# Three products of the first attention blocks moved one step in a hand-paced schedule

## The chip, the cores and the metric

One Trainium2 chip, one core of it. The metric is the device time of one execution in microseconds (us).

## The reference

An attention block feeds two feed-forward blocks. Only the first part touches the change:

```python
scores = scale * np.matmul(q, k.transpose(0, 1, 3, 2))       # B, H, S, D = 4, 8, 576, 64
bias = -(cum[:, :, :, None] - cum[:, :, None, :])            # cum: running sum of max(s, 0)
scores = np.where(causal, -1000000000.0, scores + np.minimum(bias, 0.0))
scores = scores - np.max(scores, axis=-1, keepdims=True)
attn = np.exp(scores)
attn = attn / (np.sum(attn, axis=-1, keepdims=True) + 1e-09)
out = np.matmul(attn, v)
```

The rows of `out`, 2304 tokens by 512, go through `x @ w_in`, `h - tanh(h)`, `@ w_out`, and then through `((x @ w1) * (x @ w2)) @ w3 @ w_out`.

## The kernel before, in words

Attention runs over 32 *pairs*: two heads of one batch entry, and either its first 256 query rows (kind A, one unit of work) or the other 320 (kind B, three units B1, B2, B3). The first eight pairs are batch entry 0: pairs 0 to 3 are its four A pairs, pairs 4 to 7 its B pairs. For every unit the kernel computes scores on TensorE (PE) into two PSUM banks, takes row maxima on VectorE (DVE), exponentials with row sums on ScalarE (ACT), transposes the result on PE, copies it out on ACT, and multiplies it with the values on PE (`products`, L313). The product with the values is not yet divided by the row sums. Those take their own way: `invert` (L330) makes reciprocals on DVE, `turn` (L336) transposes them on PE, `store` (L340) copies them out of PSUM on ACT (L343) and writes them to DRAM, `spread` (L347) reads them back with a DMA that repeats them over 64 partitions, into the tile `rb` (three buffers), and `finish` (L370) multiplies the two on DVE (L374), from PSUM into the tile `xy`, which the feed-forward blocks read.

The order of the work is written by hand, in steps. `at(step, order, fn, ...)` (L495) puts a piece of work into a step; pieces of a step go by their order number. A unit's scores stand in step k (order 4), its maxima in step k + 1 (order 1), its exponentials there too (2.5). Pairs 0 to 3 begin at steps 0, 2, 4, 6; pair 4 has its units at steps 8, 10, 12, pair 5 at 14, 16, 18. The products with the values of pairs 0 to 3 stand in steps 7, 9, 11, 13 at order 8, so at the end of the step. `finish` stands at order 2.6 in the step that L529 gives. Filling matmuls that compute nothing (`warm`, L213) stand in steps 1 to 12, the last nine of them in step 12 just ahead of the scores.

What this order binds differs by engine. PE runs its instructions exactly in it. ACT, DVE, GpSimd and SyncE's queue (SP) are ordered by a scheduler when the kernel is built: it plays the program through with its own estimates and lets an instruction go ahead of earlier ones if it finds it ready first. Two things hold it: data dependencies, and edges that are added by hand. `in_turn(i, other)` is such an edge: it says that i comes after `other` on its engine. `finish` puts one on its product, to `least[0]`, the last scale operation of the maxima (L261) that has been written so far. For pairs of batch entry 0, a unit's maxima end with such an operation, except B2, which takes a partial maximum that B3's step completes.

Two buffers tie `finish` to PE. For pairs 0 to 3 the products with the values go to one of two PSUM banks in turn, so pair 2's products (step 11) write the bank that pair 0's `finish` reads, and pair 3's (step 13) the bank of pair 1's:

```python
if p.first and p.early:
    p.pv = ps_y.tile([P, 512], F32, tag=f"y{p.n % 2}", name=f"pv{p.n}")
```

All other PSUM tiles of this stage (scores, transposes, reciprocals) share five banks. Pair 3's `finish` also cuts the first 256 columns of `xy` into high parts (ACT, L366) and low parts (DVE, L368), one set for each of the four pairs, which the first feed-forward block multiplies; the scheduler may run each as soon as its pair's product is there. The step of this `finish` is also what the planner takes as the begin of the first feed-forward block. Beside all this DVE and ACT convert weights, which arrive as raw 64-bit words by DMA (`raw_win`, `raw_wout`): three bit operations (L88, L91, L93), then a split into high (ACT, L64) and low part (DVE, L65).

Of the kernel before, what the change touches and what calls it, by code (L numbers as in the profile page):

```python
# [16 lines left out]
B, H, S, D = 4, 8, 576, 64  # L17
# [20 lines left out]
def tile_kernel(ctx: ExitStack, tc: tile.TileContext, qk, v, s, w_in, w_out, w1, w2, w3t, w_o2, outT):  # L38
# [84 lines left out]
    with ExitStack() as actx:  # L123
# [371 lines left out]
        def at(step, order, fn, *args):  # L495
            when.setdefault(step, []).append((order, len(when.get(step, ())), fn, args))
# [10 lines left out]
        for p in pairs:  # L507
            n, k0 = p.n, k
            lag = 5 if p.first and p.early else 7
            for m, j in enumerate(p.units):  # L510
                k = k0 + 2 * m
                for i in NEED[j]:
                    at(max(k - 2, start), 5, bias, p, i)
                    if not p.first:
                        at(max(k - 1, start + 1), 0.2, causal, p, i)
                at(k, 4, scores, p, j)
                at(k + 1, 1, minimum, p, j)
                at(k + 1, 2.5, exps, p, j)
                for e in range(2):
                    at(k + e + lag, 2, transposes, p, j, e)  # L520
                    at(k + e + lag + 1, 1.5, evacuate, p, j, e)
                at(k + lag + 2 + (not p.first), 8 if p.first else 3.9, products, p, j)
            ke = k0 + 2 * len(p.units) - 2
            k = ke + 2
            at(ke + 2, 5.5, invert, p)
            at(ke + 5, 2.4, turn, p)
            at(ke + 6, 1.2, store, p)
            at(ke + 6, 3.9, spread, p)
            fin = ke + lag + (5 if p.first and p.early else 3)  # L529
            at(fin, 2.6 if p.first else 4.05, finish, p)  # L530
            if p.hp == H // 2 - 1:
                avail.append((S * p.b + (BLK if p.early else S), fin))

            if n > 1 and (p.early or p.first):
                q = p if p.first else pairs[n + 1]
                at(max(k0 - 6, start + 1), 4.2, load, p, q, "load")
                at(max(k0 - 2, start + 1), 4.3, load, p, q, "load_v")
                if not p.first:
                    at(k0 - 5, 4.4, load, p, pairs[n + 1], "load_cum")
                    at(k0 - 3, 5.7, p.cut, pairs[n + 1])  # L540
# [529 lines left out]
```

## Time and profile before

| | |
|---|---|
| median of 3 runs | 920.8 us (920.65, 920.8, 923.38) |
| the profiled execution | 925.05 us |
| its span, first to last instruction | 923.3 us |
| mean granted TensorE clock | 0.996 |
| PE, DVE, ACT, POOL busy | 98%, 71%, 49%, 18% |
| chain that ended last, by engine | PE 80%, DVE 9%, DMA 6%, ACT 3% |

The span is one execution, followed by the hardware profiler. The chain is followed back from the last instruction: at each step to what released it, or to the instruction ahead of it on its engine. In the rows below L374 is the product in `finish`, L257 and L261 are the maxima and their scale operation, `s_B` are scores of a B pair, `pv` the products with the values, `spare` the filling matmuls. A bracket tells how long the engine had been idle before the row and what released it. PEclk 1.00 is 2.4 GHz, 0.50 is 1.2 GHz.

### The profile page before, as it was taken

The page shows a single profiled execution, that of the slowest core. Times are in us where ns is not written, and L with a number is a line of the kernel's source. Part 1 is how long each engine was busy: PE and PEld are TensorE (multiplying, and loading weights), DVE is VectorE, ACT ScalarE, POOL GpSimd, SP SyncE. Part 2 cuts the span into 40 slices and gives each one's busy share as a digit, 9 for nine tenths or more (in the row PEclk, how much of TensorE's full clock was granted, in tenths as well). Part 3 has the DMA queues.
Part 4 walks back from the last instruction along what each step waited for, and adds up shares of the span by engine and source line. Part 5 has one row for each costly group of instructions (what it writes and reads, how often), then busy time and mean ns, then how long its engine had stood idle before and what let it go on. Part 6 is the DMA issues. An engine that isn't in the chain of part 4 may idle for free.

```text
span 923.3 us, 16370 instructions
## 1 busy us (share of the span) xinstructions
PE 908.5 (98%) x6030; PEld 799.0 (87%) x6030; DVE 654.4 (71%) x1447; ACT 447.9 (49%) x1047; POOL 165.5 (18%) x170
## 2 busy tenths in 40 slices
PE   8999999999999999999999999999999999999998
PEld 5567788888888889998888888898999999999998
DVE  8787798877878766758987885867146647564555
ACT  4567888867776743334532341445224332523133
POOL 1004646554444400000000000000011111111100
PEclk9899999999999999999999999999999999999999
DMA  5655365454544523599787544346399877776874
GB/s 168 196 166 186 104 246 192 158 172 150 173 149 139 183 86 99 194 366 351 256 292 252 184 146 145 115 173 233 106 314 329 296 253 288 283 266 249 285 262 151
DMA packets 59936, 192.92 MB, mean 209 GB/s; under 512 B 6640, under 2 KB 21136, under 8 KB 55760
## 3 DMA queue, kind: packets, MB, share of 16 engines
q1 hardware_dynamic: 59856, 191.88, 60.0%
q8 instruction: 47, 0.77, 0.4%
q14 instruction: 33, 0.27, 0.1%
HBM read 148.71 MB, written 43.15 MB: 208 GB/s over the span
## 4 chain that ended last, share of the span: by engine, by line
PE 80%; DVE 9%; DMA 6%; ACT 3%; issue 1%; SPq 0%; DVEq 0%; ACTq 0%
PE h L117 10%; PE y L435 9%; PE W L875 9%; PE hb L117 9%; PE yb L117 9%; PE oW L938 5%; PE Y L875 5%; PE w3o L117 5%; PE pv L327 4%; PE oY L938 4%; PE s_B L229 4%; PE pt_B L301 3%; PE V L875 2%; DMA raw_w<-in_w3t 2%; DMA raw_wout<-in_w_out 1%
## 5 line engine op out<-in xcount | busy, mean ns | idle before, releaser
L117 PE MATMUL h<-xhl,win 128*128 128x256 f32 x864 | 120.6, 286 | 1.0 <-DVE xhl L368 0.7
L117 PEld LDWEIGHTS h<-xhl,win 128*128 128x128 f32 x864 | 105.8, 188 | 12.0 <-DVE pf_B L310 2.7
L117 PE MATMUL hb<-x,win 128*128 128x512 f32 (+1 forms) x480 | 104.5, 367 | 0.0
L117 PE MATMUL yb<-ghb,wout 128*128 128x512 f32 (+1 forms) x320 | 96.1, 368 | 1.0 <-ACT ghb L64 1.0
L117 PEld LDWEIGHTS hb<-x,win 128*128 128x128 f32 x480 | 83.9, 188 | 15.0
L206 POOL TENSOR_SCALAR pr<-cb,cq 128x384 f32<-128x384 f32 (+1 forms) x48 | 92.2, 1935 | 22.1 <-ACT pr L208 9.7
L1008 POOL TENSOR_TENSOR xy<-c,c 128x384 f32<-128x384 f32 x12 | 15.3, 1279 | 444.3 <-DVE c L997 444.3
L435 PE MATMUL y<-gh,wout 128*128 128x256 f32 x576 | 85.2, 287 | 0.9 <-DVE gh L64 0.9
L290 ACT ACTIVATE pr<-pr,nm 128x128 f32<-128x128 f32 (+2 forms) x120 | 71.5, 598 | 26.3 <-DVE nm L268 26.3
L435 PEld LDWEIGHTS y<-gh,wout 128*128 128x128 f32 x576 | 72.4, 188 | 4.2 <-issue 1.9
L117 PEld LDWEIGHTS yb<-ghb,wout 128*128 128x128 f32 x320 | 58.2, 188 | 11.5 <-ACT ghb L64 1.6
L117 PE MATMUL yb<-glb,wout 128*128 128x512 f32 (+1 forms) x160 | 58.5, 368 | 0.2 <-DVE glb L65 0.2
L301 PE MATMUL pt_B<-ident,pr 96*128 96x96 f32 (+1 forms) x384 | 50.8, 255 | 0.1
L268 DVE CUSTOM_DVE_ANT_0 pr<-s_B,pr 96x512 f32<-96x512 f32 (+1 forms) x72 | 44.3, 638 | 6.6 <-PE s_B L229 5.4
L64 ACT CAST ghb<-thb 128x512 fp32r<-128x512 f32 (+1 forms) x40 | 23.1, 578 | 50.4 <-DVE thb L737 49.7
L464 ACT ACTIVATE th<-h 128x256 f32<-128x256 f32 x72 | 26.9, 374 | 37.5 <-PE h L117 36.4
L435 PE MATMUL y<-gl,wout 128*128 128x256 f32 x288 | 45.0, 278 | 0.0
L218 POOL TENSOR_SCALAR_AFFINE_SELECT pr<-pr 128x256 f32<-128x256 f32 (+2 forms) x60 | 29.9, 521 | 82.9 <-issue 72.4
L301 PEld LDWEIGHTS pt_B<-ident,pr 96*128 96x128 f32 (+1 forms) x384 | 41.7, 143 | 2.2 <-issue 1.2
L886 ACT COPY s<-Y 128x384 f32<-128x384 f32 x24 | 11.6, 482 | 63.0 <-PE Y L875 60.6
L310 ACT COPY pf_B<-pt_B 128x512 f32<-128x512 f32 (+2 forms) x72 | 35.8, 499 | 10.0 <-PE pt_B L301 9.2
L990 DVE TENSOR_TENSOR c<-Y,u 128x384 f32<-128x384 f32 x24 | 13.3, 556 | 37.5 <-PE Y L875 37.4
(218 smaller groups left out, 2060.6 us busy)
## 6 DMA issues: line engine op xcount, KB each, us to landing
S<-wg_d SPq DMA_DIRECT2D x24, 1024.0 KB
wo<-wo_d SPq DMA_DIRECT2D x42, 512.0 KB
A<-wg_d SPq DMA_DIRECT2D x24, 768.0 KB
qk<-in_qk SPq DMA_DIRECT2D x16, 576.0 KB
raw_win<-in_w_in SPq DMA_DIRECT2D x16, 512.0 KB
raw_wout<-in_w_out SPq DMA_DIRECT2D x16, 512.0 KB
raw_w<-in_w SPq DMA_DIRECT2D x16, 512.0 KB
wg_d<-pks SPq DMA_DIRECT2D x8, 1024.0 KB
```

Source lines behind the costliest of these rows:

```text
L117: i = nc.tensor.matmul(ps, a, b, start=first and n == 0, stop=last and n == 2, skip_group_check=skip)
L206: nc.gpsimd.tensor_scalar(out=t[:pw, e, :w], in0=p.cb[:pw, e, :w], scalar1=c, scalar2=0.0, op0=ALU.add, op1=ALU.min)
L218: nc.gpsimd.affine_select(out=dg, in_=dg, pattern=[[0, 2], [-1, w - c]], compare_op=ALU.is_ge, fill=-8e9, base=0, channel_multiplier=1)
L229: latest[0] = nc.tensor.matmul(ps[e][:PW[i], o:o + k1 - k0], w[r, 0, CH0[i]:CH0[i] + PW[i]], x[r, 1, k0:k1], start=z == 0 and (not p.first ...
L268: least[0] = nc.vector.tensor_tensor_reduce(out=t[:pw, k0:k1], in0=ps[:pw, o:o + k1 - k0], in1=t[:pw, k0:k1], scale=-0.125, scalar=nm[:pw, ...
L290: last_exp[0] = nc.scalar.activation(t[:pw, :], t[:pw, :], AF.Exp, bias=m, scale=-1.0, accum_out=p.sums[:pw, e, c:c + 1])
L301: nc.tensor.transpose(pt[:, at:at + pw], p.pr[i][:pw, e, KC0[kj]:KC0[kj] + P], ident[:pw, :pw])
L310: (nc.vector.tensor_copy if j == "B2" and not p.first else nc.scalar.copy)(pf[:, :at], pt[:, :at])
L327: nc.tensor.matmul(p.pv[D * e:D * e + D, c:p.nq], p.vs[:, e, kj], pf[:, beg:end], start=z == 0, stop=z == len(todo) - 1, skip_group_check= ...
L435: nc.tensor.matmul(o, wout[f][:, z, P * c:P * c + P], x, start=f == 0 and n == 0 and c % 2 == 0, stop=f == F1 - 1 and n == 2, skip_group_c ...
L875: i = nc.tensor.matmul(ps[:, :T], w[:, x, P * j:P * j + P], b[:, y, j], start=first and j == n == 0, stop=stop and j == 1 and n == 2, skip ...
L938: nc.tensor.matmul(ps[:, :T], w[:, a, q % 2, P * j:P * j + P], x[:, b, q], start=o in ("B11", "B21", "T1") and q == z == 0, stop=o in ("T4 ...
```

## The change

The step of `finish` gets one added for the pairs whose `hp` (the pair's place in its batch entry) is below 3, if they are A pairs of batch entry 0. So pairs 0, 1 and 2 go from steps 10, 12 and 14 to 11, 13 and 15; pair 3 stays in step 16. Nothing else is edited.

```diff
-            fin = ke + lag + (5 if p.first and p.early else 3)
+            fin = ke + lag + (5 + (p.hp < H // 2 - 1) if p.first and p.early else 3)
             at(fin, 2.6 if p.first else 4.05, finish, p)
             if p.hp == H // 2 - 1:
                 avail.append((S * p.b + (BLK if p.early else S), fin))
```

Here `ke` is the step of the pair's last scores and `lag` is 5 for these pairs.

## Rows read from the trace of the kernel before

**Rows 1.** Page, part 1 (engine, busy us, share, instructions), whole span

```profile
PE 908.5 (98%) x6030; PEld 799.0 (87%) x6030; DVE 654.4 (71%) x1447; ACT 447.9 (49%) x1047; POOL 165.5 (18%) x170
```

**Rows 2.** Windows by stage, core 0 (PE, PEld, DVE, ACT, POOL busy, PEclk, DMA share, GB/s)

```profile
16.00:46.00 30.00, 27.85 (x155) 15.78 (x156) 22.54 (x58) 17.14 (x56) 0.00 (x0) 0.89 0.57 180
```

**Rows 3.** Windows of 1 us, same columns

```profile
36.00:37.00 1.00, 1.00 (x8) 0.75 (x9) 1.00 (x4) 0.00 (x0) 0.00 (x0) 0.50 0.40 158
...
42.00:43.00 1.00, 1.00 (x9) 1.00 (x8) 1.00 (x5) 0.06 (x1) 0.00 (x0) 0.61 1.02 333
```

**Rows 4.** Chain of waits, 20 to 60 us (start us, us, what)

```profile
25.19 5.16 DMA rb<-rd
...
30.90 0.60 DVE cvt_wout L91
...
53.84 6.58 DMA raw_wout<-in_w_out
```

**Rows 5.** Timeline, DVE (start us, us, engine, line, operation [idle before <-releaser])

```profile
25.29 0.41 DVE L374 TENSOR_TENSOR xy<-pv,rb 128x256 f32<-128x256 f32 x1
27.42 0.43 DVE L88 TENSOR_SCALAR cvt_wout<-raw_wout 128x512 uint32<-128x512 uint32 x1 [1.71 <-DMA raw_wout<-in_w_out]
...
30.47 0.42 DVE L374 TENSOR_TENSOR xy<-pv,rb 128x256 f32<-128x256 f32 x1 [2.03 <-DMA rb<-rd]
...
37.23 0.17 DVE L261 TENSOR_SCALAR nm<-nm 128x2 f32<-128x2 f32 x1
...
37.72 0.41 DVE L374 TENSOR_TENSOR xy<-pv,rb 128x256 f32<-128x256 f32 x1
...
41.50 1.28 DVE L257 TENSOR_REDUCE nm<-s_B 96x1 f32<-96x512 f32 x2 [1.44 <-PE s_B L245]
```

**Rows 6.** Timeline, ACT

```profile
30.93 0.41 ACT L366 CAST xhl<-xy 128x256 fp32r<-128x256 f32 x1 [3.36 <-DVE xy L374]
...
33.59 0.25 ACT L343 COPY rt<-pri 4x128 f32<-4x128 f32 x1
...
37.84 0.68 ACT L286 ACTIVATE pr<-s_B,nm 96x512 f32<-96x512 f32 x1 [3.25 <-DVE nm L261]
```

**Rows 7.** Timeline, PE

```profile
29.18 0.87 PE L327 MATMUL pv<-pf_A,vs 128*64 128x256 f32 x8
...
30.37 2.10 PE L213 MATMUL spare<-zeros,identb 128*128 128x512 bf16 x9
33.90 1.42 PE L229 MATMUL s_B<-qk 64*128 64x384 f32 x8 [1.42 <-ACT rt L343]
...
36.21 0.27 PE L245 MATMUL s_B<-maskb,identb 128*96 128x64 bf16 x1
36.41 1.55 PE L327 MATMUL pv<-pf_A,vs 128*64 128x256 f32 x8
37.89 2.80 PE L229 MATMUL s_B<-qk 64*96 64x512 f32 x4
...
48.23 1.06 PE L229 MATMUL s_B<-qk 64*128 64x384 f32 x8
...
50.06 0.21 PE L245 MATMUL s_B<-maskb,identb 128*96 128x64 bf16 x1
...
55.74 0.85 PE L435 MATMUL y<-gh,wout 128*128 128x256 f32 x6
```

**Rows 8.** Timeline, SP's queue (issues)

```profile
23.50 0.33 SPq L70 DMA_DIRECT2D raw_wout<-in_w_out  x1
...
30.05 1.10 SPq L351 DMA_DIRECT2D rb<-rd  x2
32.13 0.33 SPq L70 DMA_DIRECT2D raw_win<-in_w_in  x1
...
37.55 1.10 SPq L351 DMA_DIRECT2D rb<-rd  x2
```

## The prediction

> **What bounds the kernel now.** I read the page first. TensorE (PE) is busy 98% of the span [rows 1], so in most of the kernel a change counts only where it makes PE wait or slows PE's clock. I then cut the span into stages to find where the granted clock is below full. Only one stage stands out: 16 to 46 us, with a mean clock of 0.89 [rows 2]. Windows of 1 us show one fall, to 0.50 (the 1.2 GHz level) by 36 us, ending inside 42 to 43 us [rows 3]. The four products that the change touches all lie in this stage.
>
> The timelines show the order on each engine. VectorE (DVE) does the product of pair 0 at 25.29, of pair 1 at 30.47, of pair 2 at 37.72 [rows 5]. The reader should see the 2.03 us that DVE sat idle before the second one: it waited for `rb`, the reciprocals spread over the partitions by a DMA, and the chain of waits has that DMA ending last, 5.16 us from issue on [rows 4]. ScalarE (ACT) stood behind the same product for 3.36 us, with its high half of pair 1's columns (L366), and its copy of pair 3's reciprocals out of PSUM (L343) came only at 33.59 [rows 6]. That copy releases the PSUM bank that the scores of unit B3 (pair 4) need, so PE, done with its filling matmuls at 30.37 + 2.10 = 32.47, idled 1.42 us until 33.90 [rows 7]. The clock fell two microseconds after that gap.
>
> **The change, part by part.** It moves three DVE products in the written order and adds no instruction and no DMA. Of the three buffers of `rb`, pair 0's is wanted again by pair 3's spread, on SP's queue at 37.55 [rows 8], pair 1's and pair 2's by still later ones; the products come before these also in the new places, so SP's queue waits for nothing new. What ties each product to the new place is its ordering edge to the latest maxima's scale operation (L261) issued so far.
>
> *Pair 0, step 10 to 11.* Unit B2 in step 11 takes only a partial maximum and issues no L261, so the edge is the same one as before. Its `rb` had come. Its reader on PE's side is pair 2's products at 29.18 [rows 7], which take over its bank: 29.18 - 25.70 = 3.48 us of slack. I take 0; if it came one DVE operation later (0.6 us each, [rows 4]) the slack would still cover it.
>
> *Pair 1, step 12 to 13: what it removes.* Step 13 issues the maxima of B3, so the edge now points at B3's L261, at 37.23 before [rows 5]. The 2.03 us wait for `rb` leaves DVE's queue, and what was queued behind it runs earlier: five conversion steps and splits, then the maxima of B2. The wait of 3.36 us leaves ACT, so the copy at 33.59 comes about 2 us earlier and PE starts B3 right behind the filling matmuls, at 32.47: a gain of 33.90 - 32.47 = 1.43 us at that point. What is late next is the filling itself.
>
> *Pair 1: what it adds.* Pair 3's products on PE write the bank that pair 1's product reads. On PE they are queued directly behind B3's scores (before: scores end at 36.21 + 0.27 = 36.48, products at 36.41 [rows 7], no wait at all). Now PE must wait until DVE has done B3's maxima and the product. The price: B3's scores took 50.06 + 0.21 - 48.23 = 2.04 us in the next pair, at full clock, so they end at 34.5. (At the slower 36.48 - 33.90 = 2.58 us they end at 35.05.) In the trace the product that follows B3's maxima, pair 2's, started at 37.72, which is 1.24 us behind the end of the scores, and took 0.41 [rows 5]. So pair 1's product ends 1.65 us behind the scores, at 36.15 (or 36.7), and pair 3's products start there instead of at 36.41: 0.26 earlier, or 0.3 later. I take the first, since those scores too will run at full clock. The gap on PE has moved, from 1.42 us ahead of B3 to 1.65 us behind it. Behind the waiting products, on PE, stand the scores of B1 of pair 5, and all that follows.
>
> *What comes earlier behind it.* Half of B1's scores waited for a bank that the exponentials of B2 release. Those began at 37.84 behind B3's L261 and the first took 0.68 [rows 6], so until 38.52, against a start of B1 at 37.89 [rows 7]: at most 0.63 us of waiting. With B3's maxima some 1.9 us earlier it goes. Bounds 0 and 0.63; I take the middle, 0.3, because the half that did not wait hid a part.
>
> *Pair 2, step 14 to 15.* Its edge moves to the L261 behind B1's maxima (start 41.50 [rows 5]). Its own 0.41 us then lies in the stretch that follows B1's maxima, where the chain of waits stays on DVE until a weight DMA at 53.84 [rows 4]. I count it in full: 0.41 us. Its bank is not wanted until 55.74 [rows 7], so nothing waits for that on PE. The low half of pair 1's columns, another DVE operation of about that size, moves behind pair 1's product; DVE had 1.44 us of idle time just before 41.50 [rows 5], and I let it hide there; if it doesn't, it costs 0.41 more.
>
> *Pair 3* stays, and with it the step from which the first feed-forward block may begin. Below 0 nothing is excluded by the edges, so the lower end keeps every gain above.
>
> *The sum at the end of B1's scores and behind it:* -0.26 - 0.3 + 0.41 = -0.15 us, rounded to -0.1. Ends of these terms: -0.26 - 0.63 + 0 = -0.9 (the product of pair 2 hidden too) to 0.3 + 0 + 0.41 + 0.41 = +1.1. The orders on DVE, ACT, POOL and SP are made anew by the scheduler from its own estimate, so later stages can shift by small amounts; I allow 1 us either way for that, an estimate of two or three DVE operations. The sum stands against 925.05 us, the profiled execution (span 923.3), which is 4.25 above the median of 920.8; I carry the difference over: 920.7, own range 919 to 923. Changes up to 0.3% (2.76 us) I call no change here, about what a measurement of this kernel can tell.
>
> **The clock, and a rule beside it.** The trace shows one gap of 1.42 us and one fall behind it [rows 3, 7]. The price of the fall: 30 us at 0.89 instead of 1.00 are 3.3 us [rows 2] if PE was the bound throughout. The sum above keeps the fall, since a gap of 1.65 us takes the place of one of 1.42.
>
> The Trainium skill ("TensorE: Matmul & The Clock Gate", Part 1, on the HAM clock gate) says that the moment at which the clock switches depends on a free-running phase, so that the same kernel can differ from run to run. By it the fall would not be tied to this gap alone, and the new kernel could lose it or keep it by chance. The runs shown spread from 920.65 to 923.38, which would fit but does not show it.
>
> **Rivals.** *A, the forecast:* the wait moves from one place of PE's queue to the next, 920.7.
>
> *B, faster: the fall does not come back.* Then B1's scores run at 2.4 GHz: pair 3's products 0.87 us [rows 7] from 36.15, B1's scores 2 us (the size of B3's), so B1's maxima start at 39.1 instead of 41.50: 2.4 earlier, less 0.41 for pair 2's product, 2.0 in all, 918.8. If DVE's queue keeps all of it, the 1.43 us of the old gap and the 3.3 us of the fall come off: 4.7, 916.1. For it: DVE and ACT get work 2 us earlier, and the maxima run inside the gap. Against it: the new gap is no shorter than the old.
>
> *C, slower: pair 1's product waits for a weight.* Between B3's two L261 operations the first conversion step of a weight stood on DVE's queue. If it stands ahead of pair 1's product, the product waits for that weight's DMA, and PE behind it. It was issued at 32.13 [rows 8]. It can go at 31.15, when the two `rb` issues at 30.05 have taken their 1.10. The landing takes between 27.42 - 23.50 = 3.92 us [rows 5, 8] and 6.58 us [rows 4], so 35.1 to 37.7. It decides from a landing later than about 35.5, when B3's L261 is done. At 37.7 the product ends at 38.5 (0.34 for the step's slot and 0.41 for its own) and pair 3's products start 2.1 us later than before; with pair 2's 0.41 that is +2.5, 923.3. A gap of 4 us instead of 1.42 also makes a longer fall likely, up to another 3.3: 926.6. Against it: before, this weight had landed by the time it was wanted.
>
> *D:* the scheduler had the freedom to put pair 0's product anywhere; for pairs 1 and 2 the edges forbid the old places. That the order on the engines stays as it was is nearly excluded; the time would be 920.8.
>
> **How the numbers follow.** A 0.48, B 0.30, C 0.18, D 0.04. Of B, 2.0 to 4.7 us faster, the part beyond 2.76 is about 0.7: 0.21. Of C, 2.5 to 5.8 slower, about 0.9: 0.16. Of A the re-ordered later stages leave 0.03 beyond on each side. So faster 0.24, slower 0.19, same 0.57. The range reaches into both rivals: 916.9 leaves out about 0.09 of B, 924.8 about 0.10 of C.
>
> **What would show it.** Right: DVE no longer idles about 2 us for `rb` near 28 us; the filling matmuls and B3's scores touch on PE; a wait of 1 to 2 us stands at pair 3's products (L327), released by DVE L374; B1's maxima start between 40.5 and 41.5; the clock still reads 0.50 for some 6 us. B is shown by a full clock through 30 to 50 us with B1's maxima near 39. C is shown by a DVE wait for `raw_win` between B3's L261 and the product. The prediction is wrong if pair 3's products do not wait at all, or if most of a difference comes from behind 60 us.

## The result, and the profile after

The changed kernel takes 927.29 us (median of 6 runs, 925.93 to 929.42), the kernel before 921.04 in the same session (6 runs, 919.46 to 923.57): a ratio of 1.0055, 95% interval [1.0039, 1.0071]. It is slower by 6.2 us. The profiled execution of the changed kernel took 927.18 us, its span is 925.4 us.

The page's part 1 of the changed kernel answers to [rows 1]. It shows nothing: PE has as much to do as before.

```profile
PE 907.9 (98%) x6027; PEld 799.1 (86%) x6030; DVE 656.4 (71%) x1447; ACT 447.8 (48%) x1047; POOL 166.0 (18%) x170
```

The windows do (columns as in [rows 2]). The stage of [rows 2] has a better clock than in the profiled execution of before (0.94 against 0.89), but the next 14 us have 0.88, and PE is busy for only 10.56 of them.

```profile
16.00:46.00 30.00, 27.36 (x169) 15.86 (x170) 24.02 (x61) 17.68 (x57) 0.00 (x0) 0.94 0.58 185
46.00:60.00 14.00, 10.56 (x63) 8.20 (x65) 10.19 (x27) 8.08 (x25) 0.72 (x1) 0.88 0.56 180
...
36.00:37.00 1.00, 1.00 (x8) 0.52 (x8) 0.97 (x3) 1.00 (x4) 0.00 (x0) 0.70 0.02 9
...
39.00:40.00 1.00, 1.00 (x6) 0.66 (x5) 0.45 (x3) 0.88 (x3) 0.00 (x0) 0.60 0.75 116
...
50.00:51.00 1.00, 1.00 (x6) 0.80 (x5) 0.00 (x0) 0.14 (x1) 0.71 (x1) 0.52 0.72 290
...
53.00:54.00 1.00, 0.94 (x7) 0.75 (x5) 0.97 (x4) 0.00 (x0) 0.00 (x0) 0.77 0.47 150
```

So the clock falls to 1.2 GHz twice, each time for under 4 us: from 36.4 to 39.8, behind the moved wait, and from 50.0 to 53.5. The PE timeline of the changed kernel (columns as in [rows 7]) shows what stood ahead of each fall:

```profile
30.60 1.89 PE L213 MATMUL spare<-zeros,identb 128*128 128x512 bf16 x8
32.42 1.06 PE L229 MATMUL s_B<-qk 64*128 64x384 f32 x8
...
35.94 1.15 PE L327 MATMUL pv<-pf_A,vs 128*64 128x256 f32 x8 [1.48 <-DVE xy L374]
37.01 2.05 PE L229 MATMUL s_B<-qk 64*96 64x512 f32 x4
...
43.00 0.95 PE L117 MATMUL h<-xhl,win 128*128 128x256 f32 x6
43.79 0.52 PE L301 MATMUL pt_B<-ident,pr 128*128 128x128 f32 x4
...
48.87 1.20 PE L229 MATMUL s_B<-qk 64*128 64x384 f32 x8 [2.93 <-ACT pf_B L310]
...
54.51 1.77 PE L229 MATMUL s_B<-qk 64*96 64x512 f32 x4 [0.57 <-ACT pf_B L310]
```

The filling and B3's scores touch, and pair 3's products wait 1.48 us for pair 1's product, as forecast. What the forecast has no word for is the 2.93 us at 48.87, ahead of the scores of pair 5's B3, released by a copy on ACT. On ACT (columns as in [rows 6]) that copy stands behind a cast, the high half of a `w_in` block, which waits for DVE's conversion. The copy's own input, the transposes at 43.79 on PE, was done at 44.31, four microseconds before the copy began:

```profile
44.45 0.63 ACT L64 CAST wout<-cvt_wout 128x512 fp32r<-128x512 f32 x1
47.80 0.62 ACT L64 CAST win<-cvt_win 128x512 fp32r<-128x512 f32 x1 [2.71 <-DVE cvt_win L93]
48.32 0.50 ACT L310 COPY pf_B<-pt_B 128x416 f32<-128x416 f32 x1
```

DVE (columns as in [rows 5]) has its queue in another order too. The maxima of pair 5's B1 (40.52) stand behind pair 4's reciprocals (L333), which wait for exponentials, and behind a low half (L65); here they start 0.31 us behind the end of their scores on PE (40.21). The maxima of its B2 (46.48, 47.68) stand between the conversion steps for which ACT waits:

```profile
35.46 0.42 DVE L374 TENSOR_TENSOR xy<-pv,rb 128x256 f32<-128x256 f32 x1
...
39.46 0.17 DVE L333 TENSOR_SCALAR rw<-sums 128x6 f32<-128x6 f32 x1 [1.02 <-ACT pr L287]
39.67 0.19 DVE L334 RECIPROCAL rw<-rw 128x6 f32<-128x6 f32 x1
39.91 0.69 DVE L65 TENSOR_TENSOR win<-cvt_win,win 128x512 fp32r<-128x512 f32 x1
40.52 1.28 DVE L257 TENSOR_REDUCE nm<-s_B 96x1 f32<-96x512 f32 x2
...
46.48 0.69 DVE L257 TENSOR_REDUCE nm<-s_B 96x1 f32<-96x512 f32 x1
47.08 0.68 DVE L93 SCALAR_TENSOR_TENSOR cvt_win<-raw_win,cvt_win 128x512 uint32<-128x512 uint32 x1
47.68 0.69 DVE L257 TENSOR_REDUCE nm<-s_B 96x1 f32<-96x512 f32 x1
```

The chain of waits of the changed kernel (columns as in [rows 4]) says the same in one view. Where [rows 4] had the DMA of `rb`, there is none now; but the chain leaves PE at 34.06 and comes back to it only at 48.87.

```profile
34.06 1.28 DVE nm L257 x4
...
45.96 0.60 DVE cvt_win L91
46.56 0.60 DVE nm L257
47.16 0.61 DVE cvt_win L93
47.82 0.50 issue
48.32 0.51 ACT pf_B L310
48.87 1.20 PE s_B L229 x7
```

The instruction orders of the two built programs differ on DVE, ACT and SP's queue, up to some 70 us of the run; PE's order and everything behind are the same. So three suspects stand: the cast ahead of the copies on ACT, the new order on DVE, and the fall of the clock behind the moved wait.

### The profile page after: what moved, and what is told of

It reads as the page before. It is cut to its first block, busy times and chain, and to the rows that moved or that the text cites. A ratio compares the mean times of both kernels' runs of the same rounds, so it can differ in the third digit from the quotient of the medians.

```text
span 925.4 us, 16367 instructions
## 1 busy us (share of the span) xinstructions
PE 907.9 (98%) x6027; PEld 799.1 (86%) x6030; DVE 656.4 (71%) x1447; ACT 447.8 (48%) x1047; POOL 166.0 (18%) x170
## 4 chain that ended last, share of the span: by engine, by line
PE 80%; DVE 8%; DMA 6%; ACT 5%; issue 1%; SPq 0%; POOL 0%; ACTq 0%; DVEq 0%
PE W L875 9%; PE h L117 9%; PE y L435 9%; PE hb L117 9%; PE yb L117 9%; PE oW L938 5%; PE Y L875 5%; PE w3o L117 5%; PE pv L327 4%; PE oY L938 4%; PE s_B L229 4%; PE pt_B L301 3%; PE V L875 2%; DMA raw_w<-in_w3t 2%; DMA cb<-cum_d 1%
## 5 line engine op out<-in xcount | busy, mean ns | idle before, releaser
L736 ACT ACTIVATE thb<-hb 128x512 f32<-128x512 f32 (+1 forms) x40 | 22.2, 554 | 41.1 <-PE hb L117 40.4
```

## Experiments

The table holds all runs; each ratio is to the kernel before, with its interval. The last two columns split a kernel's executions by their mean granted clock over the span: at 0.999 or more (no fall in it), or below (0.992 to 0.998).

| kernel | median us | ratio | no fall: median (n) | fall: median (n) |
|---|---|---|---|---|
| before, again | 922.07 | 0.9997 [0.9986, 1.0008] | 921.98 (11) | 922.92 (1) |
| changed kernel | 927.29 | 1.0055 [1.0039, 1.0071] | none | 927.29 (6) |
| cast behind copies | 924.84 | 1.0027 [1.0013, 1.0040] | 924.88 (4) | 924.84 (7) |
| pair 1 alone | 924.63 | 1.0031 [1.0015, 1.0047] | none | 924.63 (12) |
| pair 2 alone | 921.90 | 0.9993 [0.9979, 1.0007] | 921.90 (12) | none |
| before, short filling | 923.14 | 1.0013 [0.9994, 1.0032] | 921.29 (5) | 924.62 (7) |
| before, cast ahead | 927.13 | 1.0051 [1.0032, 1.0069] | none | 927.13 (10) |
| changed, gap filled | 921.58 | 0.9994 [0.9978, 1.0011] | 921.58 (12) | none |
| changed, products later | 923.44 | 1.0021 [1.0001, 1.0041] | 921.78 (3) | 925.03 (9) |
| cast behind, B1's maxima first | 925.16 | 1.0029 [1.0012, 1.0045] | 922.85 (1) | 925.56 (11) |
| cast behind, both maxima first | 926.06 | 1.0034 [1.0020, 1.0048] | 922.58 (1) | 926.29 (11) |
| the same, gap filled | 921.57 | 0.9996 [0.9981, 1.0011] | 921.44 (11) | 926.05 (1) |
| before, maxima behind reciprocals | 924.29 | 1.0033 [1.0017, 1.0049] | 922.95 (2) | 925.10 (4) |

Beside these, the kernel before ran 96 times in the three sessions of the first eleven experiments (medians 922.58, 921.96, 922.28): 83 executions without a fall, 13 with one. Their medians, per session, are 922.30 (31) against 923.89 (3), 921.50 (26) against 924.18 (7), 922.21 (26) against 923.86 (3).

**The kernel before, once more.** No edit.

> The kernel before, once more, so that its runs can be laid beside the granted clock of each. Theory O (an order on ScalarE's queue costs the time: PE waits 2.93 us for a copy that stands behind a cast) says nothing on it but the level, about 921. Theory F (the clock fall near 36 us comes in some runs of the kernel before and not in others): runs with a mean clock of 0.996 lie 2 to 3 us above runs with 0.998 or more.

Its profile has no fall, so it is the better standard for what follows. Its stage row (windows, columns as in [rows 2]) reads 1.00 where [rows 2] has 0.89:

```profile
16.00:46.00 30.00, 27.66 (x167) 15.52 (x166) 24.00 (x60) 18.00 (x59) 0.00 (x0) 1.00 0.53 177
46.00:60.00 14.00, 13.25 (x94) 8.79 (x94) 11.66 (x31) 9.90 (x29) 1.46 (x2) 1.00 0.59 193
```

On PE the same wait stands at 33.90 as in [rows 7], 1.21 us long, and no clock falls behind it. The first `h` product, pair 5's B3 scores and pair 6's B1 scores follow at 43.98, 46.97 and 50.96:

```profile
33.90 1.42 PE L229 MATMUL s_B<-qk 64*128 64x384 f32 x8 [1.21 <-ACT rt L343]
...
43.98 0.95 PE L117 MATMUL h<-xhl,win 128*128 128x256 f32 x6
...
46.97 1.06 PE L229 MATMUL s_B<-qk 64*128 64x384 f32 x8
...
50.96 2.17 PE L229 MATMUL s_B<-qk 64*96 64x512 f32 x4 [0.57 <-ACT pf_B L310]
```

Against this, the changed kernel is 0.98 us *ahead* at its `h` product (43.00), in spite of its first fall, and 1.90 us behind at the B3 scores (48.87): 2.88 us are lost between these two, at the wait for the copy. At pair 6's B1 scores (54.51) it is 3.55 us behind: 1.65 us more, where the second fall, 3.4 us at half the clock, can cost up to 1.7 us. On ACT of the kernel before the copies stand ahead of the cast, which comes at 48.63:

```profile
45.22 0.62 ACT L64 CAST wout<-cvt_wout 128x512 fp32r<-128x512 f32 x1 [0.85 <-DVE cvt_wout L93]
45.75 0.50 ACT L310 COPY pf_B<-pt_B 128x416 f32<-128x416 f32 x1
...
48.63 0.62 ACT L64 CAST win<-cvt_win 128x512 fp32r<-128x512 f32 x1 [0.19 <-DVE cvt_win L93]
```

**The cast back behind the copies.** The changed kernel with one more edge (the lines that collect `casts` and `held` are not shown, here and below):

```diff
-            p.pf[j, e] = pieces, pf, at
+            p.pf[j, e] = pieces, pf, at; (p.n, j, e) == (4, "B2", 1) and in_turn(casts[held["win3"]], i)
```

> The changed kernel, with one ScalarE cast (high half of block 3 of w_in, L64) held behind the two copies L310 of pair 4's unit B2, as in the kernel before. Theory O: the 2.93 us wait of PE at 46 us falls under 0.8, pair 5's B3 scores start near 46 to 47 instead of 48.87, the clock fall at 50 us goes; 927.3 less 2.9 to 4.6 gives 922.5 to 924.5. Rival W (the wait that moved to pair 3's products, 1.48 us, and the fall behind it are the loss): within 1 us of 927.3.

The wait of 2.93 us is gone and with it half of the loss, 1.0027; the median of 924.84 lies just above what was expected of theory O. The moved wait stands as it was, 1.48 us ahead of pair 3's products. In the profiled execution no fall follows it, yet seven of the eleven executions have one. They take no more than the others: four executions without a fall take 924.88, seven with one 924.84. With so few, a difference of 1.8 us either way would not show, but the four alone lie 2.6 us above the kernel before without a fall (922.30, among the runs beside it), so most of what is left does not come from the clock. On DVE the reciprocals of pair 4 wait 1.02 us for the exponentials, and B1's maxima stand behind them at 41.11, 1.60 us behind the end of their scores (39.51 on PE). In the kernel before they start with the scores, at 40.24, the last of which end at 40.52.

```profile
40.05 0.17 DVE L333 TENSOR_SCALAR rw<-sums 128x6 f32<-128x6 f32 x1 [1.02 <-ACT pr L287]
...
40.50 0.69 DVE L65 TENSOR_TENSOR win<-cvt_win,win 128x512 fp32r<-128x512 f32 x1
41.11 1.28 DVE L257 TENSOR_REDUCE nm<-s_B 96x1 f32<-96x512 f32 x2
```

**One pair alone.** The term added to the step is `(p.hp == 1)`, then `(p.hp == 2)`, in place of `(p.hp < H // 2 - 1)`.

> Only pair 1's product is moved. The new order of the casts on ScalarE comes with it. Theory O: as the changed kernel, 926 to 928, with the wait of about 3 us at 46 us. Rival P (pair 2's product, now late in the stretch that VectorE bounds, is the loss): about 921 to 923.

> Only pair 2's product is moved; the cast stays behind the copies. Theory O: as the kernel before, 920 to 922. Rival P: 923 to 927.

Pair 1's product alone brings the cast ahead of the copies (PE waits 2.46 us at 48.01), a fall in all 12 executions, and 1.0031. That is less than theory O expected, and its time goes with the clock: the five executions with a mean clock of 0.998 take 923.49, the seven with a lower one 926.83. All six of the changed kernel are at 0.996 or below. Whether pair 1's product alone would cost the whole 0.55% is not shown. Pair 2's alone leaves the cast behind the copies, has no fall in 12 and costs nothing.

The trace of pair 2's kernel shows something else. Pair 1's product is at its old place in it, and all orders are those of the kernel before up to 37 us. But `rb` landed sooner, so DVE idled 1.09 us ahead of the product in place of 2.03, PE did not wait at B3's scores (32.42), and B1's maxima start at 38.70:

```profile
28.93 0.42 DVE L374 TENSOR_TENSOR xy<-pv,rb 128x256 f32<-128x256 f32 x1 [1.09 <-DMA rb<-rd]
...
38.70 1.28 DVE L257 TENSOR_REDUCE nm<-s_B 96x1 f32<-96x512 f32 x2 [0.20 <-PE s_B L245]
```

**The order alone, in the kernel before.** No product is moved; the copies are held behind the cast.

```diff
-            p.pf[j, e] = pieces, pf, at
+            p.pf[j, e] = pieces, pf, at; (p.n, j, e) == (4, "B2", 0) and in_turn(i, casts[held["win3"]])
```

> The kernel before with the two copies L310 of pair 4's B2 held behind the cast of block 3 of w_in, so the bad order of the changed kernel without the moved products. Theory O: PE waits 2 to 3.5 us for the copy ahead of pair 5's B3 scores near 48 us, the clock falls behind it, 925 to 928. If the order costs little without the moved wait: 922 to 923.5.

That costs 1.0051, nearly as much as the whole change, with the falls of the clock that all ten of its executions have. The scheduler lets some operations on DVE and ACT behind 48 us change places with it. The PE timeline shows the wait, the windows the clock behind it:

```profile
48.52 1.88 PE L229 MATMUL s_B<-qk 64*128 64x384 f32 x6 [1.82 <-ACT pf_B L310]
```

```profile
49.00:50.00 1.00, 1.00 (x4) 0.35 (x2) 0.00 (x0) 0.00 (x0) 0.00 (x0) 0.50 0.42 144
```

**A gap alone, in the kernel before.** Two filling matmuls instead of nine ahead of B3's scores; the order on the other engines stays.

```diff
-        at(12, 3.9, warm, 9)
+        at(12, 3.9, warm, 2)
```

> The kernel before with 2 filling matmuls instead of 9 ahead of pair 4's B3 scores; on all other engines the order is the same, and those scores start when ScalarE's copy lets them, at about 33.9 us, as before. Only PE's idle time ahead of them grows, from 1.4 to about 3 us. Theory F (what the change costs is mostly the clock, which falls when PE idles): the clock reads 0.50 for 3 us or more in nearly every run, mean clock 0.992 to 0.997, 2 to 3.5 us above the kernel before, 924 to 925.5. Rival (a fall beside stages that VectorE bounds costs nothing): 922 to 923.

This was to widen the gap at the place where the kernel before already had one. In the profiled execution it is 1.55 us and not 3, since `rb` landed sooner there too (next row, PE timeline), and no fall follows. In all, the fall comes in 7 of 12 executions, fewer than theory F expected, and those take 3.33 us longer than the other five (924.62 against 921.29). The median of 923.14 lies between the two expectations. The five without a fall are as fast as the kernel before (921.50 without a fall, among the runs beside it): in them the shorter filling costs nothing.

```profile
32.67 1.42 PE L229 MATMUL s_B<-qk 64*128 64x384 f32 x8 [1.55 <-ACT rt L343]
```

**The moved wait filled, or moved on.** In the changed kernel, seven more filling matmuls ahead of pair 3's products; or these products one step later.

```diff
-        at(12, 3.9, warm, 9)
+        at(12, 3.9, warm, 9); at(13, 6.9, warm, 7)
```

> The changed kernel with 7 filling matmuls (about 1.5 us) in the wait ahead of pair 3's products. The scheduler, which sees them too, also puts the cast of block 3 of w_in behind the copies again. Theory F: no fall, mean clock 1.0, and the time of the kernel before within 1 us, 921 to 923. Rival W (the moved wait costs by itself): the clock is 1.0, but 924 or more, as with the cast put back.

```diff
-                at(k + lag + 2 + (not p.first), 8 if p.first else 3.9, products, p, j)
+                at(k + lag + 2 + (not p.first or p.n == 3), 8 if p.first else 3.9, products, p, j)
```

> The changed kernel with pair 3's products with the values one step later, behind pair 5's B1 scores on PE, so that PE has these scores to do while VectorE does the maxima and pair 1's product. The cast goes behind the copies again. Theory F: the wait of 1.48 us at the products goes, at most 1 us remains at the B1 scores for a PSUM bank, no fall, 920 to 922.5. Rival W: the same, since the wait goes. If PE waits as long for the bank: 923 to 925.

Filled, the kernel has no fall in 12 executions and is level with the one before. But the edit did two things: the scheduler, playing the longer PE queue through, also put the cast behind the copies again and B1's maxima ahead of the reciprocals. They start at 38.99, right at the end of their scores. That is 1.25 us before those of the kernel before in the profile above, but no gain of the change: with pair 1's product at its old place they start at 38.70 (pair 2 alone), 39.01 (short filling) and 39.05 (cast ahead).

```profile
38.99 1.28 DVE L257 TENSOR_REDUCE nm<-s_B 96x1 f32<-96x512 f32 x2 [0.20 <-PE s_B L245]
...
40.19 0.16 DVE L333 TENSOR_SCALAR rw<-sums 128x6 f32<-128x6 f32 x1
```

With the products later the wait only moves again, to the scores of pair 5's B1 (next row, PE timeline). The profiled execution has no fall, but 9 of 12 have one, and it costs 925.03 - 921.78 = 3.25 us.

```profile
37.05 1.09 PE L229 MATMUL s_B<-qk 64*96 64x512 f32 x2 [1.57 <-ACT pr L286]
```

**DVE's order mended as well.** On top of the cast's edge, pair 4's reciprocals and the low half of the second `w_in` block are held behind B1's maxima; then B2's maxima too are held ahead of the conversions; then the gap is filled on top. In the diff, what is one line of code in the kernel is broken into several, and the arguments are left out.

```diff
+top = nc.vector.tensor_reduce(
...
+(p.n, j, e) == (5, "B1", 1) and [in_turn(x, top) for x in (pairs[4].inv, lows[held["win2"]])]
+least[0] = top if (p.n, j) == (5, "B2") else least[0]
```

The last line is in the second and third kernel only.

> The changed kernel with the cast behind the copies, and on VectorE the maxima of pair 5's B1 ahead of pair 4's reciprocals (L333) and of the low half of block 2 of w_in (L65), as in the kernel before. Theory D (VectorE's new order costs what the cast did not: those maxima stood 1.6 us behind the end of their scores): they start within 0.4 us of the end of the scores; 922 to 923.5 at a full clock, and now a clock fall behind the products costs up to 3.3 us where before the maxima waited anyway. Rival (the rest of the loss lies elsewhere): 924.8 as with the cast alone, at a full clock too.

> As the one before, and the maxima of pair 5's B2 too stand ahead of the conversion steps of block 3 of w_in. Theory D: 921.5 to 922.5 in runs at a full clock, 924 to 926 in runs with a fall. Rival: no change against the one before.

> As the one before, with 7 filling matmuls in the wait ahead of pair 3's products. Theory F and D together: mean clock 0.999 or 1.0 in all runs, 921 to 922, level with the kernel before or up to 1 us below it. Rival: 923 or more at a full clock, which would leave a cost of the moved products by themselves.

The medians, 1.0029 and 1.0034, show no gain from the mended orders. Nearly all executions (11 of 12 in each) now have a fall, and these take 925.56 and 926.29; the single ones without take 922.85 and 922.58, too few to show anything alone. With the gap filled 11 of 12 have none and take 921.44; here too the filling let the scheduler change places on DVE, ACT and SP, so this edit did more than fill. The twelfth, the profiled one, has a wait of 1.74 us elsewhere (45.35, for a low half of `xy`), a low clock from 46.3 to 60.0 behind it, and 926.05. One thing does not fit a fall tied to the moved wait: in the first kernel's profile the clock is full behind it (row at 37) and falls at 52 to 60 instead, behind three waits of 0.51 to 0.57 us.

```profile
36.00:37.00 1.00, 0.19 (x2) 0.20 (x4) 1.00 (x6) 0.21 (x1) 0.00 (x0) 1.00 0.86 349
37.00:38.00 1.00, 1.00 (x10) 0.61 (x8) 0.97 (x3) 1.00 (x5) 0.00 (x0) 1.00 0.01 1
...
53.00:54.00 1.00, 1.00 (x2) 0.31 (x2) 0.16 (x1) 1.00 (x5) 0.00 (x0) 0.50 0.33 120
```

**DVE's order alone, in the kernel before.** B1's maxima are held behind pair 4's reciprocals (diff broken and cut as above); no product is moved. The scheduler changes a few later places on DVE, ACT and SP with it.

```diff
+top = nc.vector.tensor_reduce(
...
+(p.n, j, c) == (5, "B1", 3) and in_turn(top, pairs[4].inv)
```

> Kernel before, with both maxima (L257) of pair 5's unit B1 held behind pair 4's reciprocals (L333, L334), as they stand in the changed kernel; no product is moved. The scheduler lets a few later operations change places with it. In the kernel before, these maxima start at 40.24 and the reciprocals at 41.45, with the last exponentials that they need done at 40.96. If VectorE's order is what remains of the loss when the cast is put back behind the copies (924.88 at full clock against 921.98), then the maxima wait for the exponentials, start at about 41.4 instead of 40.2, and the time is 1.2 to 2.9 us above the kernel before: 923.2 to 924.9 in executions whose clock does not fall. Rival: VectorE's order has slack, the time stays at 922, and what remained there is the moved wait of 1.48 us itself.

The ratio is 1.0033. The two executions without a fall take 922.95, 1.90 us over the 921.05 of the kernel before beside it (10 runs, nine of them without a fall), inside the difference that was expected of the theory, though just under the time named (the session's own level was lower). Two are few: single executions without a fall differ by more than this. The four with a fall take 925.10. The maxima start at 41.11 (DVE), and the late exponentials come back as a wait on PE of 1.33 us, where the kernel before had none:

```profile
40.80 0.17 DVE L333 TENSOR_SCALAR rw<-sums 128x6 f32<-128x6 f32 x1 [1.02 <-ACT pr L287]
...
41.11 1.24 DVE L257 TENSOR_REDUCE nm<-s_B 96x1 f32<-96x512 f32 x2
```

```profile
53.41 1.09 PE L229 MATMUL s_B<-qk 64*96 64x512 f32 x2 [1.33 <-ACT pr L286]
```

**What they show together.** Moving pair 1's product makes the scheduler choose another order. In the kernel before, the cast ahead of the copies costs 0.51% with the falls that all its executions had (none shows the order without them), and the maxima behind the reciprocals 0.33%, with falls in four of six. A fall costs 3.3 us (0.36%) in two kernels and 1.6 to 2.7 us in the kernel before, by session. The changed kernel has all three and loses 0.55%, not their sum. That they cover one another, the wait for one hiding the other, is read from the traces and not shown by a run of its own: B1's maxima stood 0.31 us behind their scores in the changed kernel, whose clock was low there, and 1.60 us in the one with the cast mended at a full clock. Nor did mending both orders help while the moved wait stayed open: nearly all those executions then had a fall. No version tried beats the kernel before; with orders and gap mended the change is level with it (0.9994 and 0.9996).

## Why the prediction was wrong

*What held.* The account of the four products, up to 43 us. Pair 1's product no longer waits for `rb`; filling and scores of B3 touch, at 32.42 (32.47 forecast). The wait went to pair 3's products, 1.48 us (1.65 forecast), which start at 35.94 (36.15 forecast). B1's maxima start at 40.52, in the window of 40.5 to 41.5 that the prediction gave. That is partly luck: a fall of the clock stands behind the wait, but it lasted 3.4 us and not the 6 that the prediction named, and the maxima stood behind other work on DVE. The price of a fall, 3.3 us, is near what two kernels measured (3.33 and 3.25) and above the 1.6 to 2.7 of the kernel before's own falls. Pair 2's term is not wrong by more than the runs can tell: alone, it costs nothing. Rival C's wait did not come: the weight was issued at 30.94 (31.15 forecast), its first conversion step stands behind the product, and DVE did not idle for it. D was rightly all but excluded.

*What failed first: "later stages can shift by small amounts; I allow 1 us either way".* This was an allowance where a mechanism was needed. In the trace ACT begins a copy whose input has been ready for four microseconds only behind the cast ahead of it. So one cast holds back two copies, and with them PE, by as much as the cast's own input is late: ACT idled 2.71 us for it, PE 2.93 us for the copy, and a fall of the clock came on top. The kernel before with this order put in lost 0.51%, falls of the clock with it. The loss lies between 43 and 55 us, so neither of the prediction's two signs of being wrong could show it. What could have been read beforehand: on ACT the copies that free the banks for PE and the casts that wait for DVE's conversions stand side by side in the queue, and on DVE the maxima beside the reciprocals. No rival was built on that; rival C looked for an operation ahead of the product on DVE, and for nothing ahead of the copies on ACT.

*What failed second: "the sum above keeps the fall" and "I carry the difference over".* The profiled execution of before had a fall of nearly 7 us [rows 2, 3] and took 925.05 us, above all three runs shown. It was the exception: 13 of 96 executions have one. To carry the difference over took the fall out of the sum on both sides, whereas in most executions the kernel before has none and the changed kernel, in all six, at least one. Had the fall been counted as brought by the change, forecast A would have been 920.7 + 3.3 = 924.0, and rival B, measured from the profile with the fall, would have had 1.4 us to win in place of 4.7.

*What failed third: the gain of 1.43 us* was read from one execution in which `rb` was late. DVE idled 2.03 us for it there and 2.16 in the second profile of the kernel before, but 1.09, 1.04 and 0.47 in three kernels whose orders are the same up to that point (pair 2 alone, short filling, cast ahead). Chains of waits give 5.16 and 5.17 us from issue to landing in the first two, 4.00 with the short filling. PE, which waited 1.42 and 1.21 us ahead of B3's scores, did not wait there at all in pair 2's kernel and the one with the cast ahead, both with all nine filling matmuls. So the wait that the change removes is not in every execution, and in the kernels with the gap filled, whose orders are mended and whose clock is full, the time is that of the kernel before within 0.2%.

What stays open is why the scheduler chose the new order: its choice is seen in the built programs, not its reasons. So does the place of each fall (below).

## What to carry to other kernels

Where a scheduler orders the queues, compare the orders of the two programs on every engine before costing a single step, and look for instructions that wait for another engine ahead of those that release the busiest one: a moved product can cost less than the cast that changes places with it. Take a profile's time as typical only after comparing it and its mean clock with the other executions. Where a wait moves on the engine whose clock falls behind waits, filling it with matmuls that compute nothing is a cheap trial, but compare the orders again, since the filling changes them too.

## What the runs showed of the hardware

The same gap is followed by a fall of the clock in some executions and not in others: the kernel before has one in 13 of 96 executions, the kernel with two fillings in 7 of 12, the one with the wait of 1.57 us in 9 of 12, the changed kernel in all 6. In the profiles, waits of 1.21 us (kernel before, second profile), 1.55 us (short filling) and 1.57 us (products later) had none behind them, in [rows 3, 7] one of 1.42 us did, and in another kernel the clock passed a wait of 1.48 us and fell 16 us later behind shorter ones. Nor is the length fixed, and it does not follow the wait: the low stretches last about 3.4 us in the changed kernel (behind waits of 1.48 and 2.93 us), nearly 7 us in [rows 3] (1.42 us), and nearly 14 us in one profile with the gap filled (1.74 us). The prediction's rival C took a longer gap to make a longer fall likely; these profiles don't bear that out.

The Trainium skill ("TensorE: Matmul & The Clock Gate", Part 1) says that the window by which the clock is switched runs freely, so that the number of slow matmuls at the start of a kernel varies from run to run. It says so of the start alone; the counts above, of falls amid a kernel, would fit it but do not show it.

What a fall costs differs too: about 3.3 us in two kernels, and no difference that can be told in the kernel with the cast mended (924.84 with, 924.88 without, seven and four executions). That another engine bounds the stretch there and hides the fall would explain the second, but is not shown.

The DMA of `rb` took 5.16 us from issue to landing in one execution and 4.00 in another, with the same orders up to there.
